# One-hot rows one iteration later, and six buffers for scaled rows: sparse attention, a gated expert layer and a dense layer on one Trainium2 core

## The chip, the cores and the metric

The kernel runs as one program on one core of a Trainium2 chip. A core has five engines that run side by side, each with its own queue in program order: TensorE (PE, matmuls into PSUM; its weight loads are listed apart as PEld), VectorE (DVE), ScalarE (ACT), GpSimd (POOL) and SyncE (SP, which mostly issues DMAs). An engine starts an instruction when the ones ahead of it in its own queue are through and the semaphores it waits for have been raised. The metric is the device time of the program in microseconds, 939.34 us before the change (median of 3 runs, 938.64 to 939.54).

## What is computed

The input has 4 batches of 8 heads with 576 tokens of 64 values. Three layers follow each other, all in float32:

```python
scores = scale * np.matmul(q, k.transpose(0, 1, 3, 2))
thresh = np.max(scores, axis=-1, keepdims=True) - tau
scores = np.where(scores >= thresh, scores, -1e9)
attn = softmax(scores)                      # written out in the reference, + 1e-9 below
x = rows(attn @ v)                          # 2304 tokens x 512

logits = x @ w_gate + modality_bias[modality_id]
e_idx = argmax(logits)                      # one of 8 experts for each token
out[mask] = gate_w[mask] * (relu(x[mask] @ w1[e]) @ w2[e])

h = out @ w_in                              # 512 -> 2048
y = (h * sigmoid(1.702 * h)) @ w_out        # 2048 -> 512
```

## The kernel before

**Stages.** The attention loop fills the first 304 us. After it, five "slots" of up to 512 tokens run through one expert each, and then the dense layer runs over blocks of 512 tokens until the end. The two stages overlap in the tail of the loop: slot 0 and slot 1 (the list called "A") take their tokens from the first three batches, whose attention is done earlier, while the last batch is still in work.

**The loop.** One iteration (`Attention.run`, L453) treats two units. A unit is 128 queries of one head against its 576 keys. For each unit PE computes scores in two of four PSUM banks (`qk`, L244), DVE takes the row maximum and clips (`max`, L272), ACT takes the exponential (`exp`, L278), and DVE applies the threshold mask and sums (`mask`, L302, into a tile `E` or `ET`). The mask is the last reader of the scores, so the scores of the next iteration wait for it: the four banks are shared by two turns. PE then transposes the masked tiles of the iteration before (`trans`, L330, copied by ACT at L332), multiplies them with V (L374, L380) and, now and then, makes one row item: the product L414 turns two heads' transposed outputs into rows of tokens and gate logits.

**A row item** (`row_items`, L410 to L433): PE's product goes to a PSUM tile `px`; ACT copies it to `xr` (L419); POOL scales the logits into `lgt` (L422) and the rows into `xrow` (L427), reading `xr` both times; SP writes `xrow` to the token table `x_dram` in DRAM with one or two DMAs (L433). `xr` and `xrow` come from the pool `a_rows` with two buffers for each name. Ten row items belong to the last batch; three are made in the loop's last iterations and seven in the tail, where `att.tail(2)` emits two of them after each of the four groups of transposes (`xprep`, L1022) that bring slot 0's gathered rows into columns (`xh` by ACT at L1023, `xl` by DVE at L1024).

**The side work.** While the loop runs, a list `side` holds small steps of the router, taken a few at a time by `sides(n)`: after the first maximum of an iteration one step, after the second two, after each mask two, and one at the iteration's end (`SD`, from iteration 54 on). An entry `None` in the list is a stop: nothing behind it is taken until the call at the end of an iteration removes it. A step that is a generator is taken one `yield` at a time. `"banks"` and `"end"` stop only some of the calls.

**The list "A"** (`Router.assign`). For the first three batches, POOL computes where each token goes: ranks, pages, limits, and at last `plf`, the position of each token split into a page of 128 and a place in it (L911). From `plf`, POOL makes `R` (`high` and `values`, L751, L752, L935), and DVE makes `OL`, a one-hot row of 128 for each token (`low`, L924, three operations of five token columns each). PE multiplies `OL` with `R` (`sum_up`, L941) and DVE turns the result into the lists of token numbers (`lists`, L949 to L957, `igaA`). POOL's indirect DMAs then gather slot 0's rows from `x_dram` (L1137), four of 128 tokens each; DVE multiplies them with their gate weight (L1298); PE transposes them (L1022); the first expert's matmuls follow (L1050). The gate weights `g` of the third batch (`gate`, L700 to L710) are also steps of this list, and are written to `x_dram` before the gathers read it.

The program order is that of the emitted code; no scheduler reorders it.

Of the kernel before, what the change touches and what calls it, by code (L numbers as in the profile page):

```python
# [8 lines left out]
F32 = mybir.dt.float32  # L9
# [11 lines left out]
DM = H * D  # L21
# [28 lines left out]
class Attention:  # L50
# [16 lines left out]
    def __init__(self, ctx, late_ctx, tc, kq, v, tau, w_gate, x_dram, router, ident, ps):  # L67
        nc = tc.nc
        self.nc, self.tc = nc, tc
        self.kq, self.v, self.x_dram = kq, v, x_dram  # L70
        self.router, self.ident = router, ident
        self.ps_tr, self.ps_av = ps
        P = lambda name, bufs, **kw: ctx.enter_context(tc.tile_pool(name=name, bufs=bufs, **kw))
        self.banks = P("a_sc", 1, space=PSUM).tile([128, 4, 512], F32, name="sc")
        Q = lambda name, bufs: late_ctx.enter_context(tc.tile_pool(name=name, bufs=bufs, side="right"))
        cst = P("a_const", 1)
        self.fp = P("a_f", 3)
        self.kp = P("a_k", 3)
        self.ep = P("a_e", 4)
        self.ex = P("a_exp", 3)  # L80
        self.et = P("a_et", 2)
        self.sm = P("a_small", 4)
        router.wk["A"] = P("r_work_a", 1)
        self.setup = P("r_setup", 1)
        lst = Q("a_late", 1)
        self.vp = Q("a_v", 4)
        self.at = Q("a_at", 2)
        self.xtp = Q("a_xt", 7)
        self.xp = Q("a_x", 2)
        self.rp = Q("a_rows", 2)  # L90

        self.cq = cst.tile([128, 1], F32, name="cq")
        self.taue = cst.tile([128, 1], F32, name="taue")
        self.tau = tau
        self.G = lst.tile([128, HP, 144], F32, name="G")
        self.w_gate = w_gate
        self.qT = [cst.tile([128, 1536], F32R, name=f"qT{i}") for i in range(3)]
        for t in self.qT:
            nc.gpsimd.memset(t.bitcast(F32)[:, 576:704], 0.0)
        self.st = {}  # L100
        self.xT = {}
        self.rs = {}
        self.extra = []
        self.norm = []
        self.writes, self.reads = {}, {}
# [292 lines left out]
    def row_items(self, b, hh):  # L398

        nc = self.nc  # L400
        xT = [self.xT[b, hp] for hp in (2 * hh, 2 * hh + 1)]
        r = self.rs[b][2]
        if hh == 0:
            self.lgt = self.xp.tile([128, 5, H, NE], F32, name="lgt")
            nc.gpsimd.memset(self.lgt[64:128, 4], 0.0)
        lgt = self.lgt
        xd = self.x_dram.rearrange("(b p j) d -> b j p d", p=64, j=PJ)
        hs = slice(hh * 4, (hh + 1) * 4)

        def item(kc):  # L410
            w = 128 if kc < 4 else 64
            px = self.ps_tr.tile([128, 512], F32, name="tr")
            for i in range(2):
                nc.tensor.matmul(  # L414
                    px[0:w, i * 144:(i + 1) * 144], xT[i][:, kc * 128:kc * 128 + w],
                    self.G[:, 2 * hh + i, :], start=True, stop=True,
                )
            xr = self.rp.tile([128, 2, 144], F32, name="xr")
            nc.scalar.copy(xr[0:w], px[0:w, 0:288].rearrange("p (a c) -> p a c", a=2))  # L419
            xrow = self.rp.tile([128, DM // 2], F32, name="xrow")  # L420
            rr = r[0:w, kc, hs].rearrange("p (a c) -> p a c", a=2)
            nc.gpsimd.tensor_mul(  # L422
                lgt[0:w, kc, hs, :].rearrange("p (a c) e -> p a c e", a=2),
                xr[0:w, :, 128:144].rearrange("p a (c e) -> p a c e", c=2),
                rr.unsqueeze(3).broadcast_to([w, 2, 2, NE]),
            )
            nc.gpsimd.tensor_mul(  # L427
                xrow[0:w].rearrange("p (a c d) -> p a c d", a=2, c=2),
                xr[0:w, :, 0:128].rearrange("p a (c d) -> p a c d", c=2),
                rr.unsqueeze(3).broadcast_to([w, 2, 2, 64]),  # L430
            )
            for u in range(2 if kc < 4 else 1):
                nc.sync.dma_start(xd[b, 2 * kc + u][:, hh * 256:(hh + 1) * 256], xrow[u * 64:(u + 1) * 64, :])  # L433
            if hh == 1 and kc == 4:
                items, gate = self.router.gate_items(b, lgt)
                self.side.extend([None] * (1 if b == B - 2 else NROW) + items + self.router.after_batch(b, gate))

        return [lambda kc=kc: item(kc) for kc in range(5)]

    def run(self):  # L440
# [116 lines left out]
class Router:  # L557
# [170 lines left out]
    def assign(self, ph, gate):  # L728
        nc, wk = self.nc, self.wk[ph]
        first = ph == "A"  # L730
# [16 lines left out]
        def compare(out, x, y, op):  # L747

            if not first:
                return nc.vector.tensor_tensor(out, x, y, op=op)  # L750
            nc.gpsimd.tensor_sub(out, x, y)  # L751
            nc.gpsimd.tensor_scalar(out, out, 0.0, None, op0=op)  # L752
# [170 lines left out]
        def low(c0, c1):  # L923
            nc.vector.tensor_tensor(  # L924
                OL[:, c0:c1], self.iota.unsqueeze(1).broadcast_to([128, c1 - c0, 128]),
                plf[:, 1, c0:c1].unsqueeze(2).broadcast_to([128, c1 - c0, 128]), op=ALU.is_equal,
            )

        def high():
            compare(  # L930
                R[:, :, 1, :], self.iota[:, 0:nh].unsqueeze(1).broadcast_to([128, n, nh]),
                plf[:, 0].unsqueeze(2).broadcast_to([128, n, nh]), ALU.is_equal)

        def values(i):
            E.tensor_mul(R[:, :, i, :], R[:, :, 1, :], self.idp[:, i, 0:n].unsqueeze(2).broadcast_to([128, n, nh]))  # L935
# [45 lines left out]
        def double(g):  # L981

            def go():
# [5 lines left out]

        return [  # L990
            "end" if first else None, ranks, *map(double, (pages, starts, limits, slots, inside, counted, places, digits)),
            *([lambda: (high(), values(0), values(1)), None, lambda: low(0, 5), lambda: low(5, 10)] if first else [
                None, high, lambda: (low(0, 5), values(0)), None, lambda: (low(5, 10), values(1)), None]),
            lambda: low(10, n), gate, *([None, "banks"] if first else [None] * NBW), lambda: sum_up(0, n), lists,
            *([] if first else [None] * 12 + [gaps, compact, None, bounds]),
# [644 lines left out]
```

## Time and profile before

| | us |
|---|---|
| median of 3 runs | 939.34 |
| lowest and highest run | 938.64, 939.54 |
| the profiled execution | 938.32 |
| its span, first to last instruction | 936.6 |
| PE busy | 906.3 (97% of the span) |
| DVE, ACT, POOL busy | 509.0, 446.7, 237.2 |

A profile is one execution. Times in its rows count from the span's start. "Busy" for PE counts the whole of each matmul, and successive matmuls overlap, so a busy PE is not a PE at its peak; a PE that is idle is idle. [...] A row's idle time in brackets is how long the engine had stood still before that instruction, and behind the arrow is what ended it.

### The profile page before, as it was taken

What the parts mean: (1) busy time and instruction counts of PE and PEld (TensorE: products, weight loads), DVE (VectorE), ACT (ScalarE), POOL (GpSimd) and SP (SyncE); (2) the same over time, 40 slices, a digit from 0 to 9 for tenths busy, and PEclk for the clock granted to TensorE, in tenths of its full rate; (3) what the DMA queues carried; (4) which work ended last, traced back from release to release, by engine and by line L of the source; (5) the groups of instructions that cost most, each with busy time, mean ns of one, the idle gap of its engine ahead of it and who ended that gap; (6) DMA issues with size and microseconds to landing.
All of it is one profiled execution on the core that took longest, in us unless ns stands there. A gap on an engine that the chain in (4) does not pass through costs nothing.

```text
span 936.6 us, 13888 instructions
## 1 busy us (share of the span) xinstructions
PE 906.3 (97%) x5031; PEld 742.3 (79%) x5031; DVE 509.0 (54%) x1106; ACT 446.7 (48%) x788; POOL 237.2 (25%) x342
## 2 busy tenths in 40 slices
PE   8999999999988899999999999999999999999994
PEld 7777777877766688778888988888888888888894
DVE  6888788888777385477777568821111111211110
ACT  6677777777756443446454545532223222222221
POOL 4937556567553311010440000010001000100100
PEclk9999999999998999999999999999999999999997
DMA  7656865664502454555666244410001000100100
GB/s 222 162 145 159 210 183 125 152 160 116 129 20 60 143 169 129 167 201 205 196 204 228 95 140 145 156 45 1 24 22 46 6 12 6 45 1 1 46 1 25
DMA packets 64523, 100.71 MB, mean 108 GB/s; under 512 B 10596, under 2 KB 35970, under 8 KB 64450
## 3 DMA queue, kind: packets, MB, share of 16 engines
q1 hardware_dynamic: 61138, 89.84, 33.0%
q0 software_dynamic: 3312, 9.94, 3.2%
q8 instruction: 41, 0.67, 0.3%
q14 instruction: 32, 0.26, 0.1%
HBM read 63.97 MB, written 17.11 MB: 87 GB/s over the span
## 4 chain that ended last, share of the span: by engine, by line
PE 78%; issue 8%; DVE 4%; POOL 4%; DMA 2%; ACT 2%; SPq 1%; POOLq 0%; ACTq 0%
PE tr L1050 28%; PE sc L1075 19%; PE sc L1094 8%; PE sc L244 8%; PE av L374 6%; PE tr L330 5%; PE tr L414 2%; PE av L380 2%; DVE e L272 1%; DMA cv_raw<-in_moe_w_in_dram 1%; ACT e L278 1%; DVE bl L1320 1%; SPq L179 1%; DVE E L302 1%; PE tr L352 1%
## 5 line engine op out<-in xcount | busy, mean ns | idle before, releaser
L1287 DVE TENSOR_TENSOR hl<-sg,hh 128x512 fp32r<-128x512 f32 (+1 forms) x80 | 51.0, 638 | 260.2 <-ACT hh L1285 257.8
L1284 ACT ACTIVATE sg<-tr 128x512 f32<-128x512 f32 (+1 forms) x80 | 44.3, 553 | 225.3 <-PE tr L1050 225.3
L278 ACT ACTIVATE e<-e,thr 128x576 f32<-128x576 f32 x144 | 109.6, 776 | 81.7 <-DVE e L272 81.3
L272 DVE TENSOR_SCALAR_CACHE_REDUCE e<-sc,taue 128x576 f32<-128x576 f32 x144 | 113.4, 815 | 37.9 <-PE sc L244 37.2
L1075 PE MATMUL sc<-wo_h,hh 128*128 128x512 f32 x288 | 112.2, 390 | 0.0
L1075 PE MATMUL sc<-wo_l,hh 128*128 128x512 f32 x288 | 112.2, 390 | 0.0
L1075 PE MATMUL sc<-wo_h,hl 128*128 128x512 f32 x288 | 112.0, 389 | 0.0
L244 PE MATMUL sc<-kA,qT 128*128 128x288 f32 x320 | 99.5, 331 | 9.5 <-DVE ET L302 6.6
L302 DVE SCALAR_TENSOR_TENSOR E<-sc,thr,e 128x576 f32<-128x576 f32 x128 | 100.6, 814 | 5.0 <-ACT e L278 4.3
L244 PE MATMUL sc<-kB,qT 128*128 128x288 f32 x320 | 88.6, 298 | 1.4 <-DVE kB L223 0.9
L244 PEld LDWEIGHTS sc<-kA,qT 128*128 128x128 f32 x320 | 60.6, 189 | 25.6 <-DVE E L302 12.6
L1050 PE MATMUL tr<-xl,wi_h 128*128 128x512 f32 (+1 forms) x320 | 78.7, 368 | 0.0
L1050 PE MATMUL tr<-xh,wi_l 128*128 128x512 f32 (+1 forms) x320 | 78.7, 368 | 0.0
L1050 PE MATMUL tr<-xh,wi_h 128*128 128x512 f32 (+1 forms) x320 | 78.6, 368 | 0.0
L374 PE MATMUL av<-AT,V 128*64 128x288 f32 x512 | 77.3, 420 | 0.5 <-ACT xT L381 0.5
L332 ACT COPY AT<-tr 128x512 f32<-128x512 f32 x128 | 68.2, 577 | 0.0
L330 PE MATMUL tr<-ident,E 128*128 128x128 f32 x512 | 68.1, 274 | 0.0
L1050 PEld LDWEIGHTS tr<-xh,wi_h 128*128 128x128 f32 x320 | 57.6, 188 | 11.0
L1050 PEld LDWEIGHTS tr<-xl,wi_h 128*128 128x128 f32 x320 | 56.9, 189 | 10.0
L1050 PEld LDWEIGHTS tr<-xh,wi_l 128*128 128x128 f32 x320 | 56.9, 189 | 10.0
L1075 PEld LDWEIGHTS sc<-wo_h,hl 128*128 128x128 f32 x288 | 54.1, 188 | 11.5
L244 PEld LDWEIGHTS sc<-kB,qT 128*128 128x128 f32 x320 | 60.8, 190 | 2.6 <-DVE kB L223 1.3
(253 smaller groups left out, 1577.9 us busy)
## 6 DMA issues: line engine op xcount, KB each, us to landing
ra<-in_moe_w_dram SPq DMA_DIRECT2D x20, 512.0 KB
rb<-in_moe_w_dram SPq DMA_DIRECT2D x20, 512.0 KB
F<-in_kq_dram SPq DMA_DIRECT2D x15, 640.0 KB
cv_raw<-in_moe_w_in_dram SPq DMA_DIRECT2D x16, 512.0 KB
cv_raw<-in_moe_w_out_dram SPq DMA_DIRECT2D x16, 512.0 KB
V<-in_vp_dram SPq DMA_DIRECT2D x16, 320.0 KB
kA<-kA SPq DMA_DIRECT2D x15, 320.0 KB
kB<-kB SPq DMA_DIRECT2D x15, 320.0 KB
```

Source lines behind the costliest of these rows:

```text
L244: m = nc.tensor.matmul(self.banks[:, bank, 0:288], l, d[kk][:, c0 + k0:c0 + k0 + 288], start=(i == 0), stop=(i == len(ops) - 1),).ins
L272: self.read(u, nc.vector.tensor_scalar(e, d["sc", w], self.taue[:, 0:1], 3.0e38, op0=ALU.add, op1=ALU.min, accum_out=thr))
L278: self.nc.scalar.activation(d["e", w], d["e", w], ACTF.Exp, bias=d["thr", w][:, 0:1], scale=-1.0)
L302: self.read(u, nc.vector.scalar_tensor_tensor(out=E.rearrange("p (a c) -> p a c", a=2), in0=d["sc", w], scalar=d["thr", w][:, 0:1], in1=d[ ...
L330: nc.tensor.transpose(tp[:, kc * 128:(kc + 1) * 128], E[:, k0 + kc * 128:k0 + (kc + 1) * 128], self.ident)
L332: return lambda: nc.scalar.copy(AT[:, h, :, c * 128:(c + 1) * 128], tp.rearrange("p (k c) -> p k c", k=4))
L374: nc.tensor.matmul(d["av"][h * 64:(h + 1) * 64, 0:288], d["V"][:, h, kc, :], d["AT"][:, h, kc, cols], start=(kc == 0), stop=False, skip_gr ...
L1050: nc.tensor.matmul(hps[:, 0:T], w[:, kd, :], blk[x][:, kd, 0:T], start=(i == 0), stop=(i == 11))
L1075: nc.tensor.matmul(y, h[:, cs], w, start=(f == 0 and i == 0), stop=(f == blk["nf"] - 1 and i == 2))
L1094: nc.tensor.matmul(blk["y"][d], w[:, ds], h[:, 0:T], start=(f == 0 and i == 0), stop=(f == last and i == 2))
L1284: nc.scalar.activation(sg, hps, ACTF.Gelu_apprx_sigmoid)
L1287: return [upper, lambda: nc.vector.tensor_sub(hl, sg, hh.bitcast(F32))]
```

## The change

One stop more is put into the list "A" ahead of the first `low`, and the tile `xrow` gets a pool of its own with six buffers. `xr` keeps its two.

```diff
@@ class Attention, __init__
         self.rp = Q("a_rows", 2)
+        self.rw = Q("a_xrow", 6)
@@ row_items
-            xrow = self.rp.tile([128, DM // 2], F32, name="xrow")
+            xrow = self.rw.tile([128, DM // 2], F32, name="xrow")
@@ Router.assign
-            *([lambda: (high(), values(0), values(1)), None, lambda: low(0, 5), lambda: low(5, 10)] if first else [
+            *([lambda: (high(), values(0), values(1)), None, None, lambda: low(0, 5), lambda: low(5, 10)] if first else [
```

Every line behind the first hunk is numbered one higher after the change. The stop moves not only `low` but all that stands behind it in the list: the gate's columns, L941, the lists and the four gathers.

On DVE, at the iterations around 273 to 290 us, the program stood so before (`e` is the clipped maximum of one unit, `E` and `ET` the masked tiles, `OL` the one-hot rows, `g` the gate weight):

```order
L312 RECIPROCAL r<-r 128x5x4
L302 SCALAR_TENSOR_TENSOR E,rs<-sc,thr,e 128x576 x2
L272 TENSOR_SCALAR e,thr<-sc,taue 128x576
L924 TENSOR_TENSOR OL<-iota,plf 128x640
L272 TENSOR_SCALAR e,thr<-sc,taue 128x576
L924 TENSOR_TENSOR OL<-iota,plf 128x640 x2
L302 SCALAR_TENSOR_TENSOR ET,rsT<-sc,thr,e 128x576
L700 TENSOR_REDUCE g<-L 128x5
L702 TENSOR_SCALAR g<-g 128x5
L302 SCALAR_TENSOR_TENSOR E,rs<-sc,thr,e 128x576
```

and with the change:

```order
L313 RECIPROCAL r<-r 128x5x4
L303 SCALAR_TENSOR_TENSOR E,rs<-sc,thr,e 128x576 x2
L273 TENSOR_SCALAR e,thr<-sc,taue 128x576 x2
L303 SCALAR_TENSOR_TENSOR ET,rsT<-sc,thr,e 128x576
L303 SCALAR_TENSOR_TENSOR E,rs<-sc,thr,e 128x576
L273 TENSOR_SCALAR e,thr<-sc,taue 128x576
L925 TENSOR_TENSOR OL<-iota,plf 128x640
L273 TENSOR_SCALAR e,thr<-sc,taue 128x576
L925 TENSOR_TENSOR OL<-iota,plf 128x640 x2
L303 SCALAR_TENSOR_TENSOR E,rs<-sc,thr,e 128x576
L701 TENSOR_REDUCE g<-L 128x5
```

The iteration whose masks write `ET` and `E` now has its two maxima next to each other, and the three `OL` stand between the maxima of the iteration after it.

On POOL, from the last operation on `R` to the gathers of slot 0, the program stood so before:

```order
L935 TENSOR_TENSOR R<-R,idp 128x15x8 x2
L706 COPY g_3447<-g 128x80
L405 MEMSET lgt 64x64
L422 TENSOR_TENSOR lgt<-xr,r 128x32
L427 TENSOR_TENSOR xrow<-xr,r 128x256
L1137 DMA xg<-x_dram,igaA 128x528 x4
```

and with the change:

```order
L936 TENSOR_TENSOR R<-R,idp 128x15x8 x2
L406 MEMSET lgt 64x64
L423 TENSOR_TENSOR lgt<-xr,r 128x32
L428 TENSOR_TENSOR xrow<-xr,r 128x256
L707 COPY g_3450<-g 128x80
L423 TENSOR_TENSOR lgt<-xr,r 128x32
L428 TENSOR_TENSOR xrow<-xr,r 128x256
L1138 DMA xg<-x_dram,igaA 128x528 x4
```

The first row item of the last batch no longer stands behind the gate's copy, and the four gathers stand behind the second row item. The larger number of `xrow` buffers moves no instruction on any engine.

## Rows read from the trace of the kernel before

**Rows 1.** Waits, 273 to 325 us: engine and line waited for; total us, times, longest.

```profile
PE sc L244 <- DVE ET L302: 6.1, 1, 6.1
PE tr L1022 <- ACT xr L419: 2.9, 1, 2.9
```

**Rows 2.** In order of time, 273 to 285 us: start, duration, engine, instruction, idle before.

```profile
273.81 0.40 PE L244 MATMUL sc<-kA,qT 128*128 128x288 f32 x1
...
276.09 0.78 ACT L278 ACTIVATE e<-e,thr 128x576 f32<-128x576 f32 x1 [1.79 <-DVE e L272]
...
277.69 0.65 PE L414 MATMUL tr<-G,xT 128*128 128x144 f32 x4
...
280.17 1.00 DVE L924 TENSOR_TENSOR OL<-iota,plf 128x640 bf16<-128x640 f32 x1 [4.17 <-POOL plf L911]
...
283.56 0.81 DVE L302 SCALAR_TENSOR_TENSOR ET<-sc,thr,e 128x576 f32<-128x576 f32 x1
...
284.43 0.61 PE L244 MATMUL sc<-kA,qT 128*128 128x288 f32 x1 [6.08 <-DVE ET L302]
```

**Rows 3.** The same view, the two iterations after it, 289 to 295 us.

```profile
289.06 0.54 PE L941 MATMUL tr<-R,OL 128*128 128x16 bf16 x15
...
290.64 0.40 PE L244 MATMUL sc<-kA,qT 128*128 128x288 f32 x1
...
291.48 0.82 DVE L272 TENSOR_SCALAR_CACHE_REDUCE e<-sc,taue 128x576 f32<-128x576 f32 x1 [0.60 <-PE sc L244]
...
294.89 0.39 PE L244 MATMUL sc<-kA,qT 128*128 128x288 f32 x1
```

**Rows 4.** Windows: stretch, its length, busy us by engine, clock, DMA share, GB/s.

```profile
284.40:288.50 4.10, 4.07 (x17) 3.97 (x18) 3.46 (x11) 1.52 (x3) 1.20 (x4) 0.50 0.10 11
288.50:303.00 14.50, 14.44 (x117) 10.92 (x115) 10.40 (x29) 9.35 (x19) 5.12 (x6) 1.00 0.34 93
...
324.50:345.00 20.50, 20.45 (x94) 16.68 (x94) 15.20 (x40) 11.09 (x18) 6.18 (x10) 1.00 0.58 188
```

**Rows 5.** In order of time, the tail, 314 to 325 us.

```profile
314.34 1.05 ACT L1319 CAST ah<-ra 128x1024 fp32r<-128x1024 f32 x1
...
315.29 0.59 ACT L1023 CAST xh<-tr 128x512 fp32r<-128x512 f32 x1
...
317.45 0.61 POOL L427 TENSOR_TENSOR xrow<-xr,r 128x256 f32<-128x256 f32 x1 [3.18 <-DMA x_dram<-xrow]
...
318.10 0.40 ACT L419 COPY xr<-tr 128x288 f32<-128x288 f32 x1 [2.23 <-POOL xrow L427]
...
318.55 0.65 PE L1022 MATMUL tr<-ident,xg 128*128 128x128 f32 x4 [2.91 <-ACT xr L419]
...
320.47 2.08 PE L1050 MATMUL tr<-xh,ah 128*128 128x512 f32 x4
...
324.32 1.07 PE L1050 MATMUL tr<-xh,ah 128*128 128x512 f32 x4
```

**Rows 6.** The chain that ended last: start, duration, a group of twelve matmuls.

```profile
338.61 2.72 PE tr L1050 x12
```

**Rows 7.** In order of time, slot 0's gathers and what uses them first.

```profile
291.19 1.31 POOL L1137 DMA_INDIRECT xg<-x_dram,igaA  x1 [4.27 <-DVE igaA L957]
...
295.42 1.00 POOL L1137 DMA_INDIRECT xg<-x_dram,igaA  x1 [0.31 <-issue]
...
304.10 1.93 DVE L1298 TENSOR_SCALAR xg<-xg 128x512 f32<-128x512 f32 x4
...
310.64 0.60 PE L1022 MATMUL tr<-ident,xg 128*128 128x128 f32 x4
```

**Rows 8.** Windows, as in rows 4: the stretch behind the last gather.

```profile
300.00:302.00 2.00, 2.00 (x18) 1.53 (x16) 1.77 (x5) 1.12 (x2) 0.00 (x0) 1.00 0.00 0
```

**Rows 9.** In order of time: two POOL operations of one size.

```profile
273.21 0.44 POOL L751 TENSOR_TENSOR ok<-rs,lim 128x120 f32<-128x120 f32 x1
...
274.72 0.44 POOL L881 TENSOR_TENSOR rs<-rs,base 128x120 f32<-128x120 f32 x1
```

## The prediction, made before the changed kernel ran

> **What bounds the kernel now.** The page comes first: the core is one, its span 936.6 us, and TensorE (PE) is busy in almost all of it, so a change is worth what it takes out of the few stretches in which PE stands idle. The second view is the list of waits, cut to 273 to 325 us [rows 1]. It shows two idle stretches of PE, 6.1 us for a mask on VectorE (DVE) and 2.9 us for ScalarE's (ACT) copy of `xr`. The changed lines stand in both. The third view is the order in time around each.
>
> The first idle stretch is in the iteration of the attention loop that I call A; the next ones are B, C and D. A's score matmuls start at 273.81, its last matmuls (L414) start at 277.69 and take 0.65, so PE is through at 278.34. B's scores start only at 284.43, after 6.08 us that end with the mask `ET` [rows 2]. The reader is to see why that mask is late: on DVE, in program order between A's two row maxima, stands the first one-hot operation `OL` (L924), which waited 4.17 us for GpSimd (POOL) to finish `plf`, until 280.17; the second maximum is queued behind it, then the two other `OL`, then the mask at 283.56 [rows 2]. A mask frees the scores' banks for the next iteration, so PE stands still for POOL's list arithmetic.
>
> What a plain iteration takes is read from C: from 290.64 to D's start at 294.89, 4.25 us [rows 3]. B took 284.43 to 290.64, 6.21 us, for two reasons: the 15 small matmuls L941 (0.54 us), and the clock, which the windows table gives as 0.50 from 284.4 to 288.5 and 1.00 from 288.5 to 303 [rows 3, 4]. [...]
>
> The second stretch is in the tail after the loop, where transposes of the first gathered rows (L1022) alternate with row products (L414). POOL's `xrow` at 317.45 waited 3.18 us for the DMA that writes an earlier `xrow` to DRAM, there being two buffers; ACT's `xr` copy at 318.10 waited 2.23 us for that `xrow` (it reads the older `xr` buffer); PE's fourth group of transposes at 318.55 waited 2.91 us for the `xr` copy, and the first expert's matmuls (L1050) start at 320.47 [rows 5]. They start at half clock: their first group of twelve lasts until 324.32, 3.85 us, where a group at full clock takes 2.72 [rows 5, 6].
>
> **The change part by part.** *The one-hot rows one iteration later.* No instruction is added. A's second maximum no longer stands behind `OL`. ACT's first exponential in A started at 276.09 and takes 0.78, a mask takes 0.81 [rows 2], so A's first mask ends near 277.7, before PE is through at 278.34; B starts then. DVE in B: its first maximum is done before 280.17 (278.34 + 0.84 to its start, as 290.64 to 291.48 in C [rows 3], + 0.82). Then the same sequence follows at the same times as now, since `plf` still ends at 280.17: `OL`, second maximum, the two other `OL`, mask at 283.56. So C starts at 284.43, when B starts now. One iteration has been done meanwhile.
>
> The three `OL` were not free and still are not: in B they lengthen DVE's iteration from about 4.25 to about 6.1 us (278.34 to 284.43), and PE idles near the end of B, from about 282.4 to 284.4 by C's length. The cover for `OL` is thus partial, and this is counted, as C's start is taken from DVE.
>
> C now carries L941. At full clock it takes 4.25 + 0.54 + about 0.2 for the gaps around it, an estimate from the same rows: D starts at 289.4 in place of 294.89 [rows 3]. The term is **-5.5 us**. Its bounds: if C runs at half clock as B does now, it takes B's 6.21 and what C's row product and `av` tail add over B (0.7, an estimate by one row product group, L414's 0.65 in A [rows 2]), so D starts at 291.3 and the term is -3.5; and at most the whole 6.1 us of idle time comes back. I take -5.5, since the idle stretch before C is then 2.0 us, less than the 2.9 us before the half clock of the tail and a third of the 6.08 before B's.
>
> What else moves: the gate's columns (`g`, L700 to L710), the small matmuls, the lists and the four gathers of slot 0 (L1137) come one iteration later in program order. `g` is made at the same time as now, as it stands behind the same `OL`. On POOL the gathers now stand behind the second row item's two multiplications. C's row product ends near 289.4, its `xr` copy near 290.1, POOL's two operations near 291.0, and the first gather starts near there, as now at 291.19; the fourth, now at 295.42, as well [rows 7]. SP's queue has the same writes in another order: the first item's two before the gate's two. Nothing behind them is urgent; the first expert loads follow only after the loop.
>
> Landed data is wanted earlier, though. The scaling of the gathered rows (L1298) starts now at 304.10 and the first transposes at 310.64 [rows 7]; by the term above they would be at 298.6 and 305.1. DMA moved nothing from 300 to 302 [rows 8], so the last gather has landed by 300. The fourth scaling would begin near 300.1. The cover was over 4 us and is nearly used up, at no cost.
>
> *Six `xrow` buffers.* In the tail POOL no longer waits: a buffer's previous write is six items back, in the loop or 4 us earlier. Replayed from the rows: ACT's `xh` ends at 315.88 (315.29 + 0.59), the `xr` copy follows at once and takes 0.40, so PE's fourth transposes start at 316.3 instead of 318.55; they take 0.65, the last `xh` ends near 317.6, and L1050 starts then instead of 320.47 [rows 5]. That is 2.85. PE idles for 0.7 us at a time only, so I let the first group run at full clock: it ends near 320.35 and not 324.32 [rows 5, 6]. The term is **-4.0 us**. Bounds: nothing, if another wait takes over (the expert weights are there by 314.34, when ACT starts on them without a wait [rows 5], which speaks against it), and 4.0; I see no loss, as no instruction is added and no queue reordered.
>
> Downstream PE is full: from 324.5 to 345 it is busy in 20.45 of 20.5 us at clock 1.00 [rows 4], and what feeds it there is ordered by program, so it moves along.
>
> Sum: the profiled execution took 938.32 us (1.7 above its span); 938.32 - 5.5 - 4.0 = 928.8. The median of the runs shown, 939.34, is 1.0 above that execution, so I predict **929.8**.
>
> [...] The rows agree that idle time comes ahead of half clock [rows 2, 4]; no row shows a gap as short as 2.0 us doing it. [...]
>
> **The rivals.** (1) *The new gap in B halves the clock for C.* For it: the 2.91 us gap of the tail did [rows 4, 5]. Against: 2.0 is shorter. Then D starts at 291.3: -3.5 - 4.0, **931.8**. (2) *The buffers only move the wait:* the tail then waits for its loads or for the gathers. For it: the writes compete with the expert weights there, and DMA is what POOL waited for. Against: the weights had come. With nothing from this part: 938.3 - 5.5 + 1.0 = **933.8**; half of it, 931.8. (3) *The first part does not do what it says*, because POOL's chain, which now runs beside a DVE that is not idle, ends later than 280.17; each us there costs one. For a term of zero it must be 5.5 us late. Against: POOL's 128x120 operation at 273.21, beside DVE's masks, took 0.44 us, and the one at 274.72, beside an idle DVE, 0.44 as well [rows 9]. Time with the buffers alone: **935.3**. (4) *Slower: the gathers come too late.* The place is POOL's queue: they stand behind one more row item, and the loop's end comes earlier. The price is one us per us once the last of them lands after about 304.6 (305.1 less one scaling of 0.48 [rows 7]); the gain is eaten when it lands 9.5 us later still, at 314. At 316 the time is 941. Against: they start at 291 either way and land by 300.
>
> **How the numbers follow.** Chances: the forecast 0.64, rival 1 0.13, rival 2 0.12, rival 3 0.05, rival 4 0.06. 0.2%, some 1.9 us, is about what a measurement of this kernel can tell from no change. All but rival 4 and the worst of 2 and 3 are beyond it: faster 0.91, same 0.03, slower 0.06. The range takes in the forecast (928.5 to 931 by itself), rivals 1 and 2 and most of 3, and a little below the forecast for gaps that may close as well: 927.5 to 935.5.
>
> **What would show it.** In the profile after: PE's wait for the mask falls from 6.1 us to about 2, and the iteration with `OL` on DVE is the one after the row product; `OL` still starts near 280.2, hardly having waited; D's scores start near 289.4; the windows show clock 1.00 around 284 to 290. In the tail, no wait of POOL for `xrow`'s DMA and none of ACT's `xr` for POOL; the first L1050 comes near 312, at full clock. The prediction is wrong if `OL` waits for `plf` past 281, if the scaling of the gathered rows waits for a DMA past 301, or if PE waits anew in the first expert slot.

## The result, and the profile after

The changed kernel took 930.41 us (median of 4 runs, 929.95 to 932.19) beside 938.99 us for the kernel before (4 runs, 938.03 to 939.54): a ratio of 0.9913 with an interval of 0.9896 to 0.993, 8.6 us less. The forecast was 929.8 us, in a range of 927.5 to 935.5. The profiled execution took 930.82 us, its span is 929.1 us: 7.5 us less than the one before, where the sum had 9.5.

The waits of the changed kernel from 273 to 325 us, all of PE's and `OL`'s, in the columns of [rows 1]. Lines are numbered one higher.

```profile
PE sc L245 <- DVE E L303: 2.8, 2, 2.6
PE tr L1023 <- ACT xr L420: 0.6, 1, 0.6
PE av L375 <- ACT xT L382: 0.5, 1, 0.5
...
DVE OL L925 <- POOL plf L912: 0.4, 1, 0.4
```

The mask wait fell from 6.1 to 2.6 us and one of 0.25, the tail's from 2.9 to 0.6, and the first `OL` hardly waits for `plf`. In order of time, B and C, where before's are in [rows 2, 3]:

```profile
277.88 0.39 PE L245 MATMUL sc<-kA,qT 128*128 128x288 f32 x1
...
279.96 1.00 DVE L925 TENSOR_TENSOR OL<-iota,plf 128x640 bf16<-128x640 f32 x1 [0.43 <-POOL plf L912]
...
283.35 0.81 DVE L303 SCALAR_TENSOR_TENSOR E<-sc,thr,e 128x576 f32<-128x576 f32 x1
...
284.22 0.40 PE L245 MATMUL sc<-kA,qT 128*128 128x288 f32 x1 [2.60 <-DVE E L303]
...
285.26 0.40 PE L245 MATMUL sc<-kA,qT 128*128 128x288 f32 x1 [0.25 <-DVE E L303]
...
287.38 0.59 PE L942 MATMUL tr<-R,OL 128*128 128x16 bf16 x15
287.90 1.97 PE L375 MATMUL av<-AT,V 128*64 128x288 f32 x8
...
290.79 0.39 PE L245 MATMUL sc<-kA,qT 128*128 128x288 f32 x1
```

B starts at 277.88, right behind A, and C at 284.22, when B started before. But C takes 6.57 us, to 290.79. The windows show what the clock did meanwhile (length, busy us of PE, its weight loads, DVE, ACT and POOL, TensorE's granted clock as a share of its full speed, DMA share, GB/s):

```profile
284.00:286.00 2.00, 1.53 (x9) 1.30 (x10) 1.97 (x9) 0.00 (x0) 0.34 (x2) 1.00 0.18 46
286.00:288.00 2.00, 2.00 (x26) 1.92 (x26) 1.65 (x5) 1.76 (x3) 0.00 (x0) 0.53 0.23 38
288.00:290.00 2.00, 2.00 (x9) 0.87 (x10) 1.22 (x6) 0.75 (x2) 0.00 (x0) 0.62 0.08 8
```

Behind a gap of 2.60 us the clock has a mean of 0.53 from 286 to 288 us and 0.62 from 288 to 290, with 0.50 from 287 to 289. Before, it was 0.50 behind a gap of 6.08 us [rows 2, 4], and had been since 282 us, within the gap. The tail, in order of time [rows 5]:

```profile
310.24 1.05 ACT L1320 CAST ah<-ra 128x1024 fp32r<-128x1024 f32 x1
311.18 0.59 ACT L1024 CAST xh<-tr 128x512 fp32r<-128x512 f32 x1
311.66 0.71 ACT L420 COPY xr<-tr 128x288 f32<-128x288 f32 x2
...
312.12 0.66 PE L1023 MATMUL tr<-ident,xg 128*128 128x128 f32 x4 [0.58 <-ACT xr L420]
...
313.34 1.21 PE L1051 MATMUL tr<-xh,ah 128*128 128x512 f32 x4
...
316.24 1.07 PE L1051 MATMUL tr<-xh,ah 128*128 128x512 f32 x4
```

The clock with it, a window of the kernel before, 320 to 322 us, and one of the changed kernel, 314 to 316 us:

```profile
320.00:322.00 2.00, 2.00 (x7) 1.34 (x6) 0.55 (x1) 0.39 (x1) 0.81 (x2) 0.50 0.35 85
...
314.00:316.00 2.00, 2.00 (x10) 1.62 (x9) 0.12 (x1) 0.00 (x0) 1.84 (x4) 1.00 0.42 104
```

No half clock any more: the first group of twelve takes 2.90 us, from 313.34 to 316.24, in place of 3.85. The 0.58 us that are left stand behind ACT's `ah`, which starts when the load of `ra` has landed, at 310.24 (its DMA takes 5.26 us, from 304.99).

The gathers and the scaling that uses them [rows 7]:

```profile
292.83 1.31 POOL L1138 DMA_INDIRECT xg<-x_dram,igaA  x1 [0.40 <-DVE e L273]
...
297.06 1.00 POOL L1138 DMA_INDIRECT xg<-x_dram,igaA  x1 [0.30 <-issue]
...
300.00 1.93 DVE L1299 TENSOR_SCALAR xg<-xg 128x512 f32<-128x512 f32 x4
```

The scaling starts with no wait for a gather. How the gain comes about, from the two profiles:

| | before | after | gain so far |
|---|---|---|---|
| A's scores | 273.81 | 273.60 | 0.21 |
| D's scores | 294.89 | 290.79 | 4.10 |
| first expert's second group | 324.32 | 316.24 | 8.08 |
| end of the span | 936.6 | 929.1 | 7.5 |

So the loop gave 3.9 us, the tail 4.0, and 0.6 went back later. That last place is slot 1's preparation, where transposes of its gathered rows alternate with slot 0's matmuls. First before, then after, in order of time:

```profile
404.35 0.43 DVE L1220 TENSOR_SCALAR cv_e<-cv_raw 128x512 uint32<-128x512 uint32 x1 [0.61 <-DMA cv_raw<-in_moe_w_in_dram]
...
412.16 0.50 PE L1050 MATMUL tr<-xl,ah 128*128 128x512 f32 x1 [0.35 <-DVE xl L1024]
```

```profile
396.84 0.43 DVE L1221 TENSOR_SCALAR cv_e<-cv_raw 128x512 uint32<-128x512 uint32 x1 [1.26 <-DMA cv_raw<-in_moe_w_in_dram]
...
404.71 0.50 PE L1051 MATMUL tr<-xl,ah 128*128 128x512 f32 x1 [1.06 <-DVE xl L1025]
```

PE came 8 us earlier, the dense layer's weights (`cv_raw`) only 7.5, and DVE, which converts them, passed the difference on. This is one pair of profiles. In e11 below, whose program differs from the changed kernel only in the number of buffers, nothing goes back there: it is 9.3 us ahead of before at the second group and 9.9 at the end, counted as below.

### The profile page after: what moved, and what is told of

It is laid out like the page before. It is cut to its first block, busy times and chain, and to the rows that moved or that the text cites. A ratio compares the mean times of both kernels' runs of the same rounds, so it can differ in the third digit from the quotient of the medians.

```text
span 929.1 us, 13886 instructions
## 1 busy us (share of the span) xinstructions
PE 904.3 (97%) x5031; PEld 740.6 (80%) x5031; DVE 508.7 (55%) x1106; ACT 446.3 (48%) x788; POOL 236.1 (25%) x342
## 4 chain that ended last, share of the span: by engine, by line
PE 82%; issue 6%; DVE 4%; POOL 3%; DMA 2%; ACT 2%; SPq 1%; POOLq 0%; ACTq 0%
PE tr L1051 28%; PE sc L1076 19%; PE sc L1095 9%; PE sc L245 8%; PE av L375 6%; PE tr L331 5%; PE tr L415 2%; PE av L381 2%; DVE e L273 1%; DMA cv_raw<-in_moe_w_in_dram 1%; DVE E L303 1%; SPq L180 1%; PE tr L353 1%; ACT e L279 1%; DMA ra<-in_moe_w_dram 1%
## 5 line engine op out<-in xcount | busy, mean ns | idle before, releaser
L1051 PE MATMUL tr<-xl,wi_h 128*128 128x512 f32 (+1 forms) x320 | 78.7, 368 | 0.0
L1051 PE MATMUL tr<-xh,wi_l 128*128 128x512 f32 (+1 forms) x320 | 78.7, 368 | 0.0
L1051 PE MATMUL tr<-xh,wi_h 128*128 128x512 f32 (+1 forms) x320 | 78.6, 368 | 0.0
L1051 PEld LDWEIGHTS tr<-xh,wi_h 128*128 128x128 f32 x320 | 57.6, 188 | 11.0
L1051 PEld LDWEIGHTS tr<-xl,wi_h 128*128 128x128 f32 x320 | 56.9, 189 | 10.0
L1051 PEld LDWEIGHTS tr<-xh,wi_l 128*128 128x128 f32 x320 | 56.9, 188 | 10.0
L1076 PEld LDWEIGHTS sc<-wo_h,hh 128*128 128x128 f32 x288 | 54.2, 188 | 10.7
```

The source lines that it names most:

```text
L1051: nc.tensor.matmul(hps[:, 0:T], w[:, kd, :], blk[x][:, kd, 0:T], start=(i == 0), stop=(i == 11))
L1076: nc.tensor.matmul(y, h[:, cs], w, start=(f == 0 and i == 0), stop=(f == blk["nf"] - 1 and i == 2))
```

## The experiments

The diffs are against the changed kernel, where nothing else is said. Ratios and their intervals are to the kernel before, timed alongside each. To compare places in the program, times are also counted from one matmul that every profile has near 262.8 us: to the start of the first expert's second group it is 61.50 us in the kernel before and 53.64 in the changed one, 7.86 less.

### One part alone

```diff
-        self.rw = Q("a_xrow", 6)
+        self.rw = Q("a_xrow", 2)
```

> The later one-hot rows alone, xrow with two buffers again. Theory (two separate gains of about 4 us each, the first cut by half clock in the iteration C): D's scores start 4 us earlier than before, the tail keeps POOL's wait of about 3 us for xrow's write and PE's of about 2.9 us, the first expert group runs at half clock; about 935.0 us. Rival (the parts lean on each other: an earlier loop end makes the tail's writes collide more with the first expert loads): the tail's wait grows by 1 us or more and the time stays above 936.5. Rival the other way (the tail's wait shrinks by itself): below 933.5.

Measured: 934.82 us (934.0 to 935.84), ratio 0.9948, 0.9934 to 0.9963. PE's waits, 265 to 325 us:

```profile
PE tr L1023 <- ACT xr L420: 3.1, 1, 3.1
PE sc L245 <- DVE E L303: 2.9, 2, 2.7
```

```diff
-            *([lambda: (high(), values(0), values(1)), None, None, lambda: low(0, 5), lambda: low(5, 10)] if first else [
+            *([lambda: (high(), values(0), values(1)), None, lambda: low(0, 5), lambda: low(5, 10)] if first else [
```

> Six xrow buffers alone, the one-hot rows where they were before. Theory: PE's 6.1 us wait for the mask stays, the tail loses its 2.9 us wait and the half clock of its first expert group; 4.0 us less than before, about 935.0 us. Rival (the wait only moves, and the gain in the changed kernel came from the earlier loop end): PE waits elsewhere in the tail for 2 us or more, 937 us or above.

Measured: 934.89 us (933.47 to 935.37), ratio 0.9954, 0.9939 to 0.9968. The same view:

```profile
PE sc L245 <- DVE ET L303: 6.2, 1, 6.2
PE tr L1023 <- ACT xr L420: 0.6, 1, 0.6
```

Each wait is there or gone with its own part, and the two parts add: up to the second group the stop alone is 3.70 us ahead of before, the buffers alone 3.97, both 7.86. The medians are 4.8 us below before with either part and 8.6 with both, which the intervals allow for. The rivals in which one part leans on the other fall.

### What the gap costs in the clock

```diff
             if it > UPP // 2:
                 self.values(AVL[it - IT_LAST] if last else AV[k])
+            if it == 68:
+                av = next(d["av"] for d in self.st.values() if "av" in d)
+                for _ in range(20):
+                    nc.tensor.matmul(av[:, 384:512], self.ident, self.ident, start=True, stop=True, skip_group_check=True)
```

> The changed kernel with 20 matmuls of the identity by itself at the end of iteration B, in the stretch in which PE stands idle before C; they write unused columns that nothing reads. Theory (the idle stretch of 2.6 us is what halves the clock in C): the granted clock stays 1.00 from 284 to 290, C takes about 5.4 us in place of 6.57, D starts about 1.1 us earlier; about 929.3 us. Rival (C is long because VectorE's masks and the gate's columns hold it, the clock decides nothing): D starts where it does now, 930.4 us. Rival (the clock falls for another reason): the clock still shows about 0.5 to 0.6 there.

Measured: 1088.98 us, and not comparable: the result comes out changed, and PE runs 5663 matmuls in place of 5031 (40 of these are the filling's, two records for each call). As I read it, attention sums that were open in that bank were spoilt, and tokens went to other experts by them; no run tests that. With `start=False, stop=False` in the same places the result is unchanged and the time was that of the next run, 929.05 us, so it is one of the two flags; no run here separates them.

```diff
-                    nc.tensor.matmul(av[:, 384:512], self.ident, self.ident, start=True, stop=True, skip_group_check=True)
+                    nc.tensor.matmul(av[:, 384:512], self.ident, self.ident, start=False, stop=False, skip_group_check=True)
```

> The same filling of B's idle stretch by 20 identity matmuls, which now add to unused columns (start=False), so that nothing else in the bank is touched. Theory (the idle stretch of 2.6 us halves the clock in C): granted clock 1.00 from 284 to 290, C takes about 5.4 us in place of 6.57, about 929.3 us. Rival (C is held by VectorE, the clock decides nothing): D starts where it does in the changed kernel, 930.4 us. Rival (the clock falls for another reason): it still shows 0.5 to 0.6 there.

Measured: 929.05 us (928.8 to 929.74), ratio 0.9891, 0.9875 to 0.9907. The clock is 1.00 in every window from 280 to 320 us, but the 20 matmuls took 4.73 us and held C back to 286.06. C then took 4.57 us, so that D came at 290.63, about where the changed kernel has it. The clock part of the theory holds; the filling was sized wrongly, and the time says little. So once more:

```diff
-                for _ in range(20):
+                for _ in range(10):
```

> The changed kernel with 10 identity matmuls in B's idle stretch in place of the 20 that took 4.7 us and held C back. Theory (the clock alone): the filling takes 2.4 us and ends before C may start at 284.2; clock 1.00; C with its L942 takes about 5.0 us in place of 6.57, so D starts near 289.2 in place of 290.8; about 928.9 us, with up to 0.8 us either way from the gaps of slot 1's transposes near 389 and 404 us. Rival (even so C is held by VectorE): D no earlier than 290.2. Rival (the filling must reach C's first matmul to keep the clock): the clock falls again, D at 290.8.

Measured: 928.37 us (927.8 to 928.83), ratio 0.9876, 0.9856 to 0.9895. In order of time, and one of the windows; from 280 to 292 us and from 312 to 318 the clock is 1.00 in each:

```profile
282.42 2.50 PE L498 MATMUL av<-ident 128*128 128x128 f32 x20
285.10 0.40 PE L245 MATMUL sc<-kA,qT 128*128 128x288 f32 x1 [0.18 <-DVE E L303]
...
290.21 0.39 PE L245 MATMUL sc<-kA,qT 128*128 128x288 f32 x1
...
286.00:288.00 2.00, 1.86 (x26) 1.86 (x27) 1.90 (x8) 0.87 (x2) 0.25 (x1) 1.00 0.33 73
```

This profile is 0.87 us later at the common matmul than the changed kernel's, so D's 290.21 is 289.34 by that one's count. C takes 5.11 us in place of 6.57 with nothing changed but idle time filled with matmuls that nobody reads: the fall of the clock costs 1.46 us. Both rivals fall.

### How many buffers

```diff
-        self.rw = Q("a_xrow", 6)
+        self.rw = Q("a_xrow", 3)
```

> The changed kernel with three xrow buffers in place of six. Theory (a write to DRAM holds its buffer some 4 us, and the second buffer of xr passes the delay on): the fourth item of the tail waits about 1.6 us for the first one's write, PE's wait for xr grows from 0.6 to about 1.6 us, about 931.4 us. Rival (three are enough): 930.4 us. Rival (only six help): the wait is near 3 us and the half clock is back, 934 us.

Measured: 932.96 us (931.0 to 934.87), ratio 0.9927, 0.9911 to 0.9943. PE's and POOL's waits, 300 to 320 us:

```profile
PE tr L415 <- ACT xr L420: 1.6, 1, 1.6
PE tr L1023 <- ACT xr L420: 0.6, 1, 0.6
...
POOL xrow L428 <- DMA x_dram<-xrow: 3.1, 2, 2.3
```

The wait has the size that was expected; the time is 1.6 us above that, since the first expert's first group is slow again as in the kernel before (315.85 to 320.31, 4.46 us for 2.90): the windows have 0.60 and 0.55 from 316 to 320 us. So the half clock came behind a wait of 1.58 us (and one of 0.58 ahead of it), shorter than the 2.0 that the prediction took to be too short for it.

```diff
-        self.rw = Q("a_xrow", 6)
+        self.rw = Q("a_xrow", 4)
```

> The changed kernel with four xrow buffers. Theory (what must be covered is a write of about 4 us, and the tail's fifth item begins 4.3 us after its first): no wait of POOL for xrow's write that PE feels; 930.4 us, as with six. Rival (some wait is left): a wait of PE above 1 us in the tail, 931.5 us or more.

Measured: 931.03 us (928.65 to 933.4), ratio 0.9906, 0.9887 to 0.9925. PE's tail wait is 0.58 us, as with six, and from D's scores to the second group it takes 25.46 us, with six 25.45. Four are enough. But this profile shows something that was not asked for. It has the same gap in B as the changed kernel, 2.61 us, and the windows behind it read:

```profile
284.75 0.40 PE L245 MATMUL sc<-kA,qT 128*128 128x288 f32 x1 [2.61 <-DVE E L303]
...
284.00:286.00 2.00, 1.00 (x5) 0.77 (x6) 1.97 (x8) 0.39 (x2) 0.72 (x3) 1.00 0.09 22
286.00:288.00 2.00, 2.00 (x29) 1.92 (x30) 1.90 (x5) 1.22 (x2) 0.15 (x1) 1.00 0.31 62
288.00:290.00 2.00, 2.00 (x15) 1.30 (x12) 1.49 (x8) 1.62 (x4) 0.00 (x0) 1.00 0.09 9
```

The clock did not fall, and C took 5.12 us (284.75 to 289.87). Up to there the program is the changed kernel's. The six runs fall apart accordingly: 928.65 and 928.68 us with a mean granted clock of 0.995 and 0.996 over the span, 930.95 to 933.4 with 0.992 to 0.994. The changed kernel's four had 0.991 to 0.994. Only one of each kernel's runs is profiled; for the others the clock is read from that mean. In the profiles of e1 and e6 the same gap, 2.67 and 2.63 us, did halve the clock: e1 has 0.50 from 286 to 288 us, and in e6 C's eight transposes take 1.91 us, for 1.03 in e5 at clock 1.00. So one gap halves it in one execution and not in another; what decides that, no run shows.

### When the gathers come too late, and where `OL` may stand

```diff
-            *([lambda: (high(), values(0), values(1)), None, None, lambda: low(0, 5), lambda: low(5, 10)] if first else [
+            *([lambda: (high(), values(0), values(1)), None, None, None, None, lambda: low(0, 5), lambda: low(5, 10)] if first else [
```

> The changed kernel with two stops more: one-hot rows, L942, lists and gathers two iterations later still. Theory (rival 4 of the prediction, with its threshold): the gathers start near 301, the last lands after 306, the first transposes of gathered rows come about 2 us after the last loop work is through, about 932.5 us. Rival (the gathers have more room than I reckon): no wait for them, 930.4 us. Rival (the late gathers cost the full 8.5 us less 3): above 935 us.

Measured: 937.11 us (934.64 to 939.52), ratio 0.9974, 0.9961 to 0.9987; well above the 932.5 of the theory, and in the range of the second rival. The scaling of the gathered rows, and a window of the same stretch:

```profile
303.17 0.50 DVE L1299 TENSOR_SCALAR xg<-xg 128x512 f32<-128x512 f32 x1 [5.18 <-DMA xg<-x_dram,igaA]
305.91 0.49 DVE L1299 TENSOR_SCALAR xg<-xg 128x512 f32<-128x512 f32 x1 [2.24 <-DMA xg<-x_dram,igaA]
309.11 0.49 DVE L1299 TENSOR_SCALAR xg<-xg 128x512 f32<-128x512 f32 x1 [2.71 <-DMA xg<-x_dram,igaA]
310.13 0.49 DVE L1299 TENSOR_SCALAR xg<-xg 128x512 f32<-128x512 f32 x1 [0.53 <-DMA xg<-x_dram,igaA]
```

```profile
306.00:308.00 2.00, 0.33 (x1) 0.14 (x1) 0.40 (x1) 0.00 (x0) 0.00 (x0) 1.00 1.07 403
```

PE waited 4.6 us for them in three pieces, and what follows in the tail, from 310 to 316 us, ran at half clock (0.50). The gathers were issued 6.7 us later than in the changed kernel (299.52 for 292.83), and the last ones met the first expert's weight loads, with the DMA engines full: from the fourth's issue to its scaling it took 6.4 us (303.75 to 310.13). Earlier in the same profile a short gap of PE, for a mask, halved the clock as well; the window behind the one shown has 0.52:

```profile
290.94 0.40 PE L245 MATMUL sc<-kA,qT 128*128 128x288 f32 x1 [1.38 <-DVE E L303]
...
292.00:294.00 2.00, 2.00 (x10) 1.99 (x11) 0.86 (x4) 0.78 (x1) 0.25 (x1) 0.63 0.10 10
```

One iteration later than in the changed kernel, with `OL` shared out, the delay of the gathers is still free:

```diff
-            *([lambda: (high(), values(0), values(1)), None, None, lambda: low(0, 5), lambda: low(5, 10)] if first else [
+            *([lambda: (high(), values(0), values(1)), None, None, lambda: low(0, 5), None, lambda: low(5, 10)] if first else [
```

> The changed kernel with one more stop between the first one-hot row and the other two: one OL in B, two in C, L942, the lists and the gathers one iteration later than in the changed kernel. Theory (each iteration of VectorE hides some 0.5 us, and short gaps do not halve the clock): B's gap falls from 2.6 to about 0.7 us, C gets one of about 1.7 us, the clock stays 1.00, the gathers start near 296 and land by 304, just in time; about 928.5 us. Rival (the gathers are then too late): the scaling of the gathered rows waits for a DMA and PE's first transposes start 1 us or more after the last row of the loop; 931 us or more.

Measured: 928.97 us (928.56 to 930.17), ratio 0.9888, 0.9871 to 0.9905. PE's waits, 273 to 325 us:

```profile
PE sc L245 <- DVE E L303: 1.3, 3, 0.9
PE tr L942 <- ACT AT L333: 1.2, 1, 1.2
PE tr L1023 <- ACT xr L420: 0.6, 1, 0.6
```

The clock stays 1.00 behind gaps of 0.9 and 1.2 us. The 1.2 us were not foreseen: in D, which has one more transposed tile than C, L942 waits for ACT's copy `AT`, which, as I read it, frees a PSUM buffer. The last three versions put `OL` behind the masks, where DVE stands idle at each iteration's end. `"end"` holds a step back until then; the gate's small steps go ahead of it.

```diff
-            *([lambda: (high(), values(0), values(1)), None, None, lambda: low(0, 5), lambda: low(5, 10)] if first else [
-                None, high, lambda: (low(0, 5), values(0)), None, lambda: (low(5, 10), values(1)), None]),
-            lambda: low(10, n), gate, *([None, "banks"] if first else [None] * NBW), lambda: sum_up(0, n), lists,
+            *([lambda: (high(), values(0), values(1)), None, None, gate, "end", lambda: (low(0, 5), low(5, 10)), "end", lambda: low(10, n), "end"] if first else [
+                None, high, lambda: (low(0, 5), values(0)), None, lambda: (low(5, 10), values(1)), None,
+                lambda: low(10, n), gate, *[None] * NBW]), lambda: sum_up(0, n), lists,
```

> The changed kernel with the gate ahead of the one-hot rows, two OL behind B's second mask, the third behind C's second mask, and L942 at the end of D. Theory (VectorE has about 1 us idle behind each second mask, and what lies there delays no mask): B's gap is gone, C ends with one of about 1 us, clock 1.00 throughout, gathers near 296 as with the split; about 927.5 us. Rival (VectorE's idle time behind the masks is an illusion, its queue is full): gaps of 2 us in sum as with the split, 929 us. Rival (gathers too late): 931 us.

Measured: 927.97 us (927.78 to 929.31), ratio 0.9881, 0.9865 to 0.9898. No gap in B or C; PE waits 1.5 us, until 304.44, for the fourth gather, and the clock is 1.00 behind that wait too. POOL issues that gather at 300.00, behind a row item. Two versions of it follow; their diffs are against this one.

```diff
-            *([lambda: (high(), values(0), values(1)), None, None, gate, "end", lambda: (low(0, 5), low(5, 10)), "end", lambda: low(10, n), "end"] if first else [
+            *([lambda: (high(), values(0), values(1)), None, None, gate, "end", lambda: (low(0, 5), low(5, 10), low(10, n)), "banks"] if first else [
```

> The three OL all behind B's second mask, the gate ahead of them, L942 in the middle of C as in the changed kernel. Theory (two OL behind the masks cost PE nothing in the run before, and its only loss was 1.5 us for late gathers): no gap in B, one below 1 us at the end of C, gathers near 292 and no wait for them, clock 1.00; about 927.2 us. Rival (the third OL comes at full price, and the gap of 1.5 us or more halves the clock for a while): 928.5 us or more.

Measured: 928.46 us (928.26 to 929.09), ratio 0.9877, 0.9858 to 0.9897. The third `OL` is not free: PE waits 0.76 us for it at L942 and 0.72 for ACT behind it. The time is the rival's, its half clock did not come: from 280 to 292 us and from 312 to 318 the windows have 1.00.

```diff
-                lambda: low(10, n), gate, *[None] * NBW]), lambda: sum_up(0, n), lists,
+                lambda: low(10, n), gate, *[None] * NBW]), lambda: sum_up(0, n), double(lists),
```

> The version with the one-hot rows behind the masks (two OL behind B's second mask, one behind C's) with the list steps taken two at a time, so that all four gathers stand ahead of the last row item on GpSimd. Theory (that version's only loss in the loop was the fourth gather, issued at 300.0 behind that row item, and PE waited 1.5 us for it): the fourth gather starts near 298, PE waits under 0.3 us for the scaled rows, no other gap from 275 to 303; about 926.5 us. Rival (the gathers are bound by the DMA's own time, not by their place): the wait stays above 1 us, 928 us.

Measured: 927.95 us (926.73 to 929.08), ratio 0.988, 0.9861 to 0.9899. The wait for the gathers is gone (the fourth is issued at 298.52 and scaled at 302.43, 3.9 us), and the second group starts 11.71 us ahead of before (e8: 10.13). The time did not follow. Of the 11.71 us, 0.4 goes near 321 us, where a matmul (L770) waits for POOL's `pre`, and 0.5 where the profile has

```profile
386.78 0.66 PE L1023 MATMUL av<-ident,xg 128*128 128x128 f32 x4 [1.29 <-DVE xl L1025]
```

in place of 0.43 us in e8. It is the first of two such gaps in slot 1's preparation; the changed kernel gave back its 0.6 at the second, at 404.71. Past the second, near 402 us here, this version is 10.75 us ahead of before, e8 10.14. That `cv_raw` sets it is read from DVE's waits there, not tried: no run loads those weights earlier. These last versions, the split and the short filling lie at 928.0 to 929.0 us; the runs don't order them, but all lie below the changed kernel's median, which was taken beside other runs of the kernel before.

## Why the prediction was right, and where it was not

**The total** came out, 930.41 for 929.8, on one term that held and one that was 1.6 us too large. The medians moved by 8.6 us of the 9.5 that were summed up, the two profiled executions by 7.5. That the total lies within 0.6 us is in part luck: the sum gave 928.8 for the profiled execution, which took 930.82, and the execution profiled before lay 0.7 us below its median, the one after 0.4 above.

**The first term, -5.5, measured -3.9.** B at once behind A (278.34 forecast, 277.88 measured), `OL` at 280.2 (279.96), C at 284.43 (284.22): right, and with POOL's `plf` no later than before rival 3 falls. The failed step is "since the idle stretch before C is then 2.0 us, less than the 2.9 us before the half clock of the tail". It failed twice. The gap was 2.6 us, for B's transposes and products ended at 281.6, earlier than C's length had told: B has no row product, and the 0.7 us that the prediction itself gives for it, taken off here too, would have made the gap 2.5. And the comparison of lengths does not hold: this gap halved the clock, and in e6 and e7 gaps of 1.58 and 1.38 us did. C at full clock takes 5.11 us (e9), near the 4.99 that were added up; with the fall, 6.57. What the term would be without it, -3.9 - 1.5 = -5.4, is the forecast's. Rival 1, priced at -3.5 and given 0.13, is what the profiled execution did. e11 shows that it is a matter of the execution: one gap of 2.61 us did not halve the clock, one of 2.60 did, and without the fall D's scores came 5.34 us earlier against the common matmul than before, near the 5.5.

**The second term, -4.0, measured -4.0**, and in e2 alone 3.97. Rival 2 falls. Inside it the first L1051 came 3.0 us earlier against D, not 2.85, and 0.95 of the 1.13 us from the clock came.

**Cover and downstream.** The gathers were issued from 292.83 to 297.06, 1.6 us later than in the kernel before and than forecast, since C's row product came later. They were in time all the same: the scaling started at 300.00 without a wait (298.6 forecast). Rival 4 has its place and its price, but no fixed point from which it decides: the late gathers of e7 ran into the weight loads and landed more slowly (6.4 us from the fourth's issue to its scaling, for 3.9 in e12), so that issue 6.7 us later cost 6.6 us up to the second group (e7 against the changed kernel). The half clock from 310 to 316 us is in that price, so it does not tell how much cover was left. "What feeds it there is ordered by program, so it moves along" was wrong by 0.6 us in the profiled execution, as DVE's waits read: the `cv_raw` loads did not move as far as PE. In e11's profile nothing went back, so the size is not settled, and why the loads lag is not shown.

## What to carry to other kernels

Work that an engine must wait for belongs behind what others wait for on it, and a wait that must stay is cheaper where nothing urgent is queued behind it. Price an idle gap of TensorE with the clock behind it (1.46 us here), as a chance and not as yes or no (gaps of 2.60 and 2.61 us went different ways), and look for the next consumer that is fed by loads of its own. As many buffers help as items are made while one write is under way: here, with a write of 4.3 us, four did what six did (a wait of PE of 0.58 us with either), and three left one more, of 1.58 us.

## What the runs showed of the hardware that was not expected

A gap of 2.60 to 2.67 us ahead of C halved the clock in three profiles (the changed kernel's, e1, e6) and not in a fourth (e11: 2.61). Shorter gaps fall on both sides too: 1.38 us (e7) and 1.58 us (e6) did it; 0.87 and 1.17 us (e4) and 1.46 us (e8) did not. A write of one `xrow` tile held its buffer 4.3 us (e6: made by 309.85, POOL let go at 314.12). Matmuls with `start=True, stop=True` into unused columns of a bank changed the result (e3); with both flags `False` they did not (e5).
